# Linear attention beside an MLP: the kv blocks in 60-feature groups on half tiles, and the last rows of M copied by two DMA queues

## The chip, the cores and the metric

The kernel runs on one core of a Trainium2 chip. The metric is the device time of one execution in microseconds, from the start of the program to its end. The kernel before takes 263.5 us, the median of 3 runs that lie between 263.39 and 263.82 us.

The core has four engines that compute: TensorE (PE in the profile, its weight loads PEld), VectorE (DVE), ScalarE (ACT) and GpSimd (POOL). A fifth, SyncE (SP), only issues transfers. SP, ACT and POOL can each start DMA transfers from their own instruction stream, and each engine runs its own stream in order. Semaphores are the only tie between the engines.

## The reference: what is computed

There is one input x of 2048 tokens by 640 features in bfloat16. Two branches use it, and a gate per token mixes them.

```python
def _A_ref(x, wqkv, wo):                       # H = 32 heads of Dh = 20 features
    qkv = ((x @ wqkv).reshape(B, S, 3, H, Dh)).transpose(2, 0, 3, 1, 4)
    q, k, v = qkv[0], qkv[1], qkv[2]
    phi = lambda t: jnp.where(t > 0, t + 1, jnp.exp(t)) + 1e-6
    pq, pk = phi(q), phi(k)
    kv = jnp.einsum("bhsd,bhse->bhde", pk, v)  # one 20 x 20 block per head
    z = jnp.einsum("bhsd->bhd", pk)
    num = jnp.einsum("bhqd,bhde->bhqe", pq, kv)
    den = jnp.einsum("bhqd,bhd->bhq", pq, z)[..., None] + 1e-6
    return (num / den).transpose(0, 2, 1, 3).reshape(B, S, D) @ wo

def _B_ref(x, w1, w2, w3, w4):                 # F = 1728
    h = _gelu(_layernorm(x) @ w1)
    # four quarters of h are shifted by 1, -1, 2, -2 tokens
    x1 = x + shifted(h) @ w2
    return x1 + _gelu(_layernorm(x1) @ w3) @ w4

g = _sigmoid((x * gate_w).sum(-1, keepdims=True))
return g * a + (1 - g) * b
```

## The kernel before, in words

**Branch A without a pass over the values.** The kernel never forms v. Since kv = pk^T (x wv), it first builds GT, the 640 x 640 product of x and pk over the tokens (`gt_step`, L795), and then multiplies it with wv. Only the 20 x 20 blocks on the diagonal of that product are wanted, one per head. Then the blocks of kv are folded into the output projection: M is the block-diagonal kv times wo, 640 x 640, so that the attention output of a token tile is one matrix product of the normalised pq with M (`a_tile`).

**The kv stage.** `kvt_group` (L950) makes the diagonal of the product in groups of R6 = 120 features, that is six heads: five groups of 120 and one of 40. Each group is 5 matmuls over the contraction, 30 in all, in two work items ("kvt", 0) and ("kvt", 1) of 20 and 10. A matmul loads 128 columns of wv as its weights and moves 120 columns of GT. `lt_evac` multiplies each group in PSUM with a mask of 20 x 20 blocks on VectorE and writes it to Lt. For each of the six groups `m_group` (in order 5, 0, 1, 2, 3, 4) then makes 120 rows of M with two matmuls, of 512 and 128 columns (L613 with Lt and wo_aug as operands), and ScalarE copies them out of PSUM (L669).

**Where the last 40 rows of M go.** The five 120-row groups fill partitions 0 to 119 of the five blocks of `M_sb`. The 40 rows of group 5 go to partitions 120 to 127 of the blocks, eight to each. An engine cannot move rows across partitions, so ScalarE copies group 5 to `Mt`, and `m_tail` (item ("mt",)) copies it from there by 5 DMAs of 8 rows each on SP's queue (L286). `a_tile` for token tile 0 waits for all of them. `qn_scale` writes the normalised pq in the same order of features (L1063), and `qt_tile` turns it to features by tokens with a DMA transpose on SP (L282).

**What sets the order.** Every operation is recorded by a small scheduler. The work is cut into items with costs, streams and dependencies; a planner (`_Items.run`) picks the next item by the earliest time that its model gives, and so writes out a fixed order for every engine before the program runs. Waits between engines follow from the memory that operations read and write. PSUM has eight banks, and `bank` and `pair` hand out the ones that the model expects to be free first; `bank_hold` keeps banks from being handed out. SP's stream is one queue in that order: the DMA transposes of the normalised tokens ("t1", u) and ("t2", u), those of pq ("qt", t), the five copies of ("mt",), the weight loads and the stores. ("t2", u) waits for GpSimd's normalisation of tile u (L635), and that waits for a slot of the three-deep buffer xn, so for the transpose three tiles earlier.

**The stretch around the change.** After GT, PE does the first MLP of branch B (w1 with xnT, w2 with hsT) and then the second (w3 with xnT into h2T, w4). The kv matmuls stand among the w1 groups, the M matmuls among the w2 and w3 groups. A w3 group is 5 matmuls of 512 columns (`w3_group`) that ScalarE empties with a gelu. Twenty w3 groups stand before the first `a_tile`; after it `a_tile` 1 to 3 alternate with further w3 groups.

**Half tiles elsewhere in the kernel.** `w3_half` (L1036) already runs two matmuls side by side, each on 64 of the 128 columns of the array, and `w4_half` (L1104, L1101) two matmuls on 64 of the 128 rows each.

Of the kernel before, what the change touches and what calls it, by code (L numbers as in the profile page):

```python
# [21 lines left out]
NK = D + 4  # L22
R6 = 120

# [405 lines left out]
def _build(nc, A_x, A_wqkv, A_wo, B_w1, B_w2, B_w3, B_w4, gate_w, out, dbg=None, stop=None):  # L430
# [49 lines left out]
    ident = pa.alloc("ident", [128, 128], BF16)  # L480
    mask = pa.alloc("mask120", [128, 6, 20], BF16)
    mask_t = pa.alloc("mask_t", [128, 6, 20], BF16)
    negh = pa.alloc("negh", [128, 4], F32)
# [86 lines left out]
    def nfree(ap):  # L570
        n = 1
        for d_ in ap.shape[1:]:
            n *= d_
        return n
# [96 lines left out]
    def memset(engf, ap, val):  # L671
        return engf(lambda e: e.memset(ap, val), [], [ap])
# [63 lines left out]
    memset(pool, negh[:], -0.5)  # L736
    aselect(mask_t[0:120], ones_c[0:120, 0:120].rearrange("p (b d) -> p b d", b=6), [[-20, 6], [0, 20]], ALU.is_ge, 0, 1)
    aselect(mask[0:120], mask_t[0:120], [[20, 6], [0, 20]], ALU.is_ge, 19, -1)
# [194 lines left out]

    kv_bank = {}

    def kvt_group(h):
        b = pair()
        kv_bank[h] = b
        bank_hold.update((b, b + 1))
# [12 lines left out]
        pe(fn, [wvf[:, :], GT[:, :, :]], [ps[:, b, 0:480], ps[:, b + 1, 0:1]], cost=len(mms) * 60.0)  # L952

    def lt_evac(h):
        b = kv_bank[h]
        for q_, r in enumerate(range(4) if h == 0 else range(4, 6)):
            n = min(R6, D - R6 * r)
            src = ps[0:n, b, R6 * q_:R6 * q_ + n].rearrange("p (h m i) -> p h m i", m=5, i=4)
            msk = mask[0:n, 0:n // DH, :].rearrange("p h (m i) -> p h m i", i=4)
            if r < 5:  # L960
                dst = Lt[0:n, r, 0:n].rearrange("p (h m i) -> p h m i", m=5, i=4)
            else:
                dst = Lt[0:n, r, 0:n].rearrange("p (m h i) -> p h m i", m=5, i=4)
            tt(dve, dst, src, msk, ALU.mult)
        bank_hold.difference_update((b, b + 1))

    def m_group(r):
        n = min(R6, D - R6 * r)
        kr = R6 if r < 5 else 128
        b = pair()  # L970
        mm_group(ps[:, b, 0:512], [(Lt[0:kr, r, :], wo_aug[0:kr, r, 0:512])])
        mm_group(ps[:, b + 1, 0:128], [(Lt[0:kr, r, :], wo_aug[0:kr, r, 512:D])])
        src = psf[0:n, 512 * b:512 * b + D]
        dst = M_sb[0:n, r, :] if r < 5 else Mt[0:n, :]
        activation(dst, src, ACTF.Copy)

    def m_tail():
# [73 lines left out]
    def qn_scale(t):  # L1051
        sd = qn_slot[t]
        ts(dve, dnr[:, 0, sd, :], dnr[:, 0, sd, :], EPS_PHI, None, ALU.add, ALU.bypass)
        dve(lambda e: e.reciprocal(dnr[:, 1, sd, :], dnr[:, 0, sd, :]), [dnr[:, 0, sd, :]], [dnr[:, 1, sd, :]], cost=350.0)
        blk = pq_tok[:, t, :].rearrange("p (j c) -> p j c", c=128)
        main = (blk[:, :, 0:R6].rearrange("p j (a d) -> p j a d", d=DH),
                pq_tok[:, t + 1, 0:5 * R6].rearrange("p (j a d) -> p j a d", a=6, d=DH),
                dnr[:, 1, sd, 0:30].rearrange("p (j a) -> p j a", a=6).unsqueeze(3).to_broadcast([128, 5, 6, DH]), 850.0)
        tail = (blk[:, :, R6:128].rearrange("p m (h i) -> p h m i", i=4),
                pq_tok[:, t + 1, 5 * R6:D].rearrange("p (h m i) -> p h m i", h=2, i=4),  # L1060
                dnr[:, 1, sd, 30:32].unsqueeze(2).unsqueeze(3).to_broadcast([128, 2, 5, 4]), 150.0)
# [114 lines left out]
    IT.add("MISC", ("w3load",), 0.0, w3_load, deps=[(("k", NT - 1), 0.0), (("t1", NT - 1), 0.0)])  # L1176
    IT.add("MISC", ("w4load",), 0.0, w4_load, deps=[(("kvt", 1), 0.0), (("t1", NT - 1), 0.0), (("z", NT - 1), 1.5)])
    for c in range(NCH):
        for j in range(KFF):
            deps = []  # L1180
            if c == 0 and j == 0:
                deps0 = [(("kvt", 1), 0.0), (("z", NT - 1), 1.5)]
            else:
                deps0 = []
# [95 lines left out]
```

## Time and profile before

| what | value |
|---|---|
| median of 3 runs | 263.5 us |
| the profiled execution, its own time | 263.69 us |
| its span from the first to the last instruction | 261.6 us |
| DVE busy | 149.0 us, 57% of the span |
| ACT busy | 106.8 us, 41% |
| POOL busy | 95.3 us, 36% |
| DMA, mean | 95 GB/s |
| granted TensorE clock | 1.000 |

A row of the timeline gives start, duration, engine, line, operation and tiles, then how many instructions were merged; in brackets stands the idle time before it and what ended it. A row of SPq or ACTq is the issue of a transfer, and its duration is the time that the issuing queue was occupied, not the time until the data landed. The chain of waits is the list of pieces that led to the last instruction, in order of time. L613, L643, L669 and L286 are lines of helpers that record matmul groups, VectorE tensor operations, ScalarE activations and transfers, so a row of theirs is told apart by its tiles. A matmul's duration in a row includes the way through the array; the pace is read from the starts.

### The profile page before, as it was taken

To read this page: it belongs to the slowest core of one execution; us is meant where nothing else is said; L and a number is where in the kernel's file an instruction comes from. 1 tells how busy PE (TensorE), PEld (TensorE's weight loads), DVE (VectorE), ACT (ScalarE), POOL (GpSimd) and SP (SyncE) were. 2 spreads that over 40 slices of the span, in tenths; PEclk is the share of its full clock that TensorE was granted. 3 is DMA by queue.
4 is the path that set the end of the run, shared out by engine and by line. 5 is a ranking of instruction groups with operands and counts; after the bars stand their busy time and mean duration, and the time that the engine had idled before them with its cause. 6 is when DMAs were issued, how large, how long until landed. Compare 5 with 4: busy or idle time off the path is not lost.

```text
span 261.6 us, 4268 instructions
## 1 busy us (share of the span) xinstructions
PE 256.0 (98%) x1668; PEld 135.7 (52%) x1699; DVE 149.0 (57%) x267; ACT 106.8 (41%) x215; POOL 95.3 (36%) x150
## 2 busy tenths in 40 slices
PE   8999999999999999999999999999999999999996
PEld 4555555555555555554444545554455544455553
DVE  2497787899903699979995407992023410143332
ACT  1386767752355756684875140005500045100000
POOL 5003996849774018687753201230011100011000
PEclk9999999999999999999999999999999999999999
DMA  6885979660566895544766600232000020000211
GB/s 198 253 91 137 165 172 172 179 122 16 87 125 103 224 387 155 76 81 74 111 124 125 103 0 0 41 84 77 0 3 0 3 100 0 3 0 0 103 50 50
DMA packets 50612, 24.82 MB, mean 95 GB/s; under 512 B 41973, under 2 KB 49182, under 8 KB 50593
## 3 DMA queue, kind: packets, MB, share of 16 engines
q1 hardware_dynamic: 49152, 20.98, 36.6%
q0 software_dynamic: 1152, 3.28, 5.7%
q8 instruction: 13, 0.21, 0.3%
q10 hardware_dynamic: 288, 0.30, 0.3%
q14 instruction: 7, 0.05, 0.1%
HBM read 12.04 MB, written 2.62 MB: 56 GB/s over the span
## 4 chain that ended last, share of the span: by engine, by line
PE 95%; DVE 1%; DMA 1%; issue 1%; ACT 0%
PE ps L613 60%; PE ps L1122 21%; PE ps L795 8%; PE ps L874 2%; DMA x_tok<-in_A_x_dram 1%; PE ps L1036 1%; PE ps L1104 1%; DVE x_tok L652 1%; PE ps L875 1%; PE ps L624 1%; PE ps L950 1%; DVE abx L652 0%; ACT junk L668 0%; DVE xT L678 0%; PE ps L1101 0%
## 5 line engine op out<-in xcount | busy, mean ns | idle before, releaser
L613 PE MATMUL ps<-xnT,w 128*128 128x512 bf16 x348 | 80.7, 379 | 0.7 <-issue 0.2
L1122 PE MATMUL ps<-w,h2T 128*128 128x512 bf16 (+1 forms) x411 | 58.1, 298 | 0.3
L669 ACT ACTIVATE h2T<-ps 128x512 bf16<-128x512 f32 x52 | 30.4, 600 | 65.7 <-PE ps L613 65.7
L613 PEld LDWEIGHTS ps<-xnT,w 128*128 128x128 bf16 x360 | 34.0, 98 | 36.9 <-issue 0.4
L652 DVE SCALAR_TENSOR_TENSOR x_tok<-ps,stg,abx 128x512 bf16<-128x512 f32 (+1 forms) x32 | 17.2, 550 | 61.6 <-PE ps L1122 61.6
L635 POOL TENSOR_SCALAR abx<-x_tok,stg 128x640 f32<-128x640 bf16 x16 | 14.8, 927 | 101.9 <-DVE x_tok L652 95.1
L1122 PEld LDWEIGHTS ps<-w,h2T 128*128 128x128 bf16 x416 | 32.4, 98 | 25.6 <-issue 1.1
L635 POOL TENSOR_SCALAR xn<-x_tok,st 128x640 bf16<-128x640 bf16 x32 | 33.8, 1062 | 15.3 <-DMA xnT<-xn 14.8
L669 ACT ACTIVATE Er<-ps 128x640 bf16<-128x640 f32 x32 | 22.3, 705 | 18.7 <-PE ps L875 8.6
L668 ACT ACTIVATE junk<-x_tok 128x640 bf16<-128x640 bf16 x32 | 23.6, 737 | 4.8 <-DVE x_tok L650 4.3
L669 ACT ACTIVATE hsT<-ps 128x512 bf16<-128x512 f32 (+1 forms) x32 | 18.9, 594 | 15.1 <-PE ps L613 14.8
L613 PE MATMUL ps<-M_sb,pqnT 128*128 128x512 bf16 (+1 forms) x157 | 23.7, 297 | 0.2
L613 PE MATMUL ps<-w,hsT 128*128 128x128 bf16 (+1 forms) x158 | 23.7, 298 | 0.1
L795 PE MATMUL ps<-pk_tok,x_tok 128*128 128x128 bf16 (+1 forms) x156 | 23.3, 297 | 0.2
L652 DVE SCALAR_TENSOR_TENSOR abx<-ps,stg,abx 128x640 f32<-128x640 f32 x16 | 14.1, 884 | 14.6 <-PE ps L613 14.6
L613 PE MATMUL ps<-wkg,xT 128*128 128x131 bf16 (+1 forms) x148 | 22.4, 298 | 0.1
L613 PEld LDWEIGHTS ps<-w,hsT 128*128 128x128 bf16 x160 | 13.3, 98 | 12.3
L613 PEld LDWEIGHTS ps<-M_sb,pqnT 128*128 128x128 bf16 x160 | 13.1, 98 | 10.4
L613 PE MATMUL ps<-wq,xT 128*128 128x128 bf16 (+1 forms) x118 | 18.1, 298 | 0.1
L650 DVE SCALAR_TENSOR_TENSOR x_tok<-ps,x_tok 128x640 bf16<-128x640 f32 x16 | 13.1, 821 | 6.9 <-PE ps L613 6.0
L613 PEld LDWEIGHTS ps<-wkg,xT 128*128 128x128 bf16 x150 | 12.2, 98 | 9.0
L795 PEld LDWEIGHTS ps<-pk_tok,x_tok 128*128 128x128 bf16 x160 | 12.4, 98 | 8.4
(70 smaller groups left out, 231.8 us busy)
## 6 DMA issues: line engine op xcount, KB each, us to landing
w<-in_B_w_dram SPq DMA_DIRECT2D x1, 2160.0 KB, 8.5
w<-in_B_w_dram SPq DMA_DIRECT2D x1, 2080.0 KB, 14.1
x_tok<-in_A_x_dram SPq DMA_DIRECT2D x3, 640.0 KB, 5.8
out_dram<-x_tok SPq DMA_DIRECT2D x3, 640.0 KB, 3.5
w<-in_B_w_dram POOLq DMA_DIRECT2D x8, 160.0 KB, 5.1
wkg<-in_A_wqkv_dram SPq DMA_DIRECT2D x5, 160.0 KB, 4.1
wv<-in_A_wqkv_dram POOLq DMA_DIRECT2D x1, 800.0 KB, 6.2
wo_aug<-in_A_wo_dram POOLq DMA_DIRECT2D x5, 150.0 KB, 5.2
```

What stands on the lines that cost most here:

```text
L613: ins = e.matmul(out_ap, l, r, start=(i == 0), stop=(i == n - 1))
L624: ins = e.transpose(o, s_, ident[:])
L635: return engf(lambda e: e.tensor_scalar(out_ap, in_ap, s1, s2, op0, op1), rd, [out_ap], cost=cost)
L650: return dve(lambda e: e.scalar_tensor_tensor(out_ap, in0, scalar, in1, op0, op1, accum_out=accum), rd, [out_ap, accum], cost=cost + 70.0)
L652: return dve(lambda e: e.scalar_tensor_tensor(out_ap, in0, scalar, in1, op0, op1), rd, [out_ap], cost=cost)
L668: return act(lambda e: e.activation(out_ap, in_ap, func, bias=bias, scale=scale, accum_out=accum), rd, wr, cost=cost)
L669: return act(lambda e: e.activation(out_ap, in_ap, func, bias=bias, scale=scale), rd, wr, cost=cost)
L795: ins = e.matmul(o, l, r, start=(t0 + q_ == 0), stop=(t0 + q_ == NT - 1))
L874: e.matmul(ps[:, b, 0:512], l, w[:, k, 0:512], start=(k == 0), stop=(k == KD - 1))
L875: return e.matmul(ps[:, b + 1, 0:n2], l, w[:, k, 512:512 + n2], start=(k == 0), stop=(k == KD - 1))
L950: ins = e.matmul(o, l, r_, start=st_, stop=sp_, skip_group_check=True)
L1122: ins = e.matmul(o, l, r, start=False, stop=(i == KFF - 1), skip_group_check=(n0 > 0))
```

## The change

The features are taken in groups of R3 = 60 (three heads) instead of 120: ten groups of 60 and one of 40. Two groups stand side by side, one on partitions 0 to 59 and one on 64 to 123; `PAIRS` names them.

- `kvt_group` becomes one item of 55 matmuls, of 64 columns of weights each: 50 that move 60 columns and 5 that move 40. The two groups of a pair write the two halves of the same PSUM bank, and all six pairs share one bank.
- `lt_evac` becomes four VectorE multiplications in place of six.
- Lt holds four slots of 60 columns and one full slot; `m_group` is used for group 5 and for slot 4 (all 128 rows). The other eight groups are done by the new `m_quads`: 16 matmuls on tiles of 64 x 64, eight of 512 columns and eight of 128. They take six single PSUM banks, held together, and ScalarE empties them with four copies of 512 columns and two of 256.
- M has groups of 60 rows and then 4 rows from group 5 in each half of a block. `m_tail` so becomes ten DMAs of 4 rows, five on SP's queue and five on ACT's, alternating, and depends on ("mq",) instead of on ("m", 5), since the copies out of PSUM now write all 128 partitions of M_sb.
- `load_wvo` loads wo by seven DMAs on GpSimd's queue in place of six, and the whole of wo_aug is set to zero at the start (3840 columns in place of 640). The mask is made by four selects and one addition in place of two selects.
- `qn_scale` writes 10 x 60 and 10 x 4 features in place of 5 x 120 and 5 x 8.

The core of the diff:

```diff
-R6 = 120
+R3 = 60
+PAIRS = ((0, 2), (1, 3), (4, 6), (5, 7), (8, 9), (10,))
...
     def load_wvo():
...
-        for r in range(6):
-            n = min(R6, D - R6 * r)
-            sch.dma("pool", wo_aug[0:n, r, :], A_wo[R6 * r:R6 * r + n, :], "wo", group_total=6, deps=dp)
+        for c, r, g, m in ((0, 0, 0, 2), (1, 0, 2, 2), (0, 2, 4, 2), (1, 2, 6, 2), (0, 4, 8, 1), (1, 4, 9, 1)):
+            sch.dma("pool", wo_aug[64 * c:64 * c + R3, r:r + m, :],
+                    A_wo[R3 * g:R3 * (g + m), :].rearrange("(g p) d -> p g d", p=R3), "wo", group_total=7, deps=dp)
+        sch.dma("pool", wo_aug[0:D - 10 * R3, 5, :], A_wo[10 * R3:D, :], "wo", group_total=7, deps=dp)
...
-    memset(pool, wo_aug[:, 5, :], 0.0)
     memset(pool, hsT[:, :, 0:4], 0.0)
     memset(pool, hsT[:, :, S:S + 4], 0.0)
+    memset(pool, wo_aug[:], 0.0)
...
-    def kvt_group(h):
-        b = pair()
...
+    def kvt_group():
+        b = bank()
+        kv_bank.append(b)
+        bank_hold.add(b)
         mms = []
-        for q_, r in enumerate(range(4) if h == 0 else range(4, 6)):
-            n = min(R6, D - R6 * r)
+        for r, gs in enumerate(PAIRS):
             for k in range(KD):
-                mms.append((ps[:, b, R6 * q_:R6 * q_ + n], wvf[:, D * k + R6 * r:D * k + R6 * r + 128], GT[:, k, R6 * r:R6 * r + n],
-                            q_ == 0 and k == 0, k == KD - 1))
+                for c, g in enumerate(gs):
+                    n = min(R3, D - R3 * g)
+                    mms.append((ps[64 * c:64 * c + 64, b, R3 * r:R3 * r + n], wvf[:, D * k + R3 * g:D * k + R3 * g + 64],
+                                GT[:, k, R3 * g:R3 * g + n], r == 0 and k == 0, k == KD - 1))
...
+    def m_quads():
+        held = [bank() for _ in range(6)]
+        bs, bt = held[:4], held[4:]
+        bank_hold.update(held)
...
+        for i in range(2):
+            jobs = []
+            for h in range(2):
+                rows = slice(64 * h, 64 * h + 64)
+                for c in range(2):
+                    jobs.append((ps[64 * c:64 * c + 64, bs[2 * i + h], :], Lt[rows, 2 * i + c, 0:64],
+                                 wo_aug[rows, 2 * i + c, 0:512], True))
+            quad(jobs, [ps[:, bs[2 * i + h], :] for h in range(2)])
...
+        for j in range(4):
+            activation(M_sb[:, j, 0:512], ps[:, bs[j], :], ACTF.Copy)
+        for h in range(2):
+            activation(M_sb[:, h:4:2, 512:D], ps[:, bt[h], 0:256].rearrange("p (i n) -> p i n", n=128), ACTF.Copy)
+        bank_hold.difference_update(held)
+
     def m_tail():
-        for j in range(KD):
-            sch.dma("sp", M_sb[R6:128, j, :], Mt[8 * j:8 * j + 8, :], "mt", group_total=KD)
+        for s_ in range(2 * KD):
+            p0 = 64 * (s_ % 2) + R3
+            sch.dma(("sp", "act")[s_ % 2], M_sb[p0:p0 + 4, s_ // 2, :], Mt[4 * s_:4 * s_ + 4, :], "mt", group_total=2 * KD)
...
-    for h in range(2):
-        IT.add("KVF", ("kvt", h), 0.0, lambda h=h: kvt_group(h), deps=[(("g", KD - 1), 1.0)])
-        IT.add("KVF", ("lt", h), 0.0, lambda h=h: lt_evac(h), deps=[(("kvt", h), 0.0)])
-    for n, r in enumerate((5, 0, 1, 2, 3, 4)):
-        IT.add("KVF", ("m", r), 0.0, lambda r=r: m_group(r), deps=[(("lt", 1), 1.0), (("w3", (1 + 3 * n) // KFF, (1 + 3 * n) % KFF), 0.0)])
-    IT.add("MT", ("mt",), 0.0, m_tail, deps=[(("m", 5), 1.5), (("t1", NT - 1), 0.0)])
+    IT.add("KVF", ("kvt",), 0.0, kvt_group, deps=[(("g", KD - 1), 1.0)])
+    IT.add("KVF", ("lt",), 0.0, lt_evac, deps=[(("kvt",), 0.0)])
+    IT.add("KVF", ("m", 5), 0.0, lambda: m_group(5), deps=[(("lt",), 1.0), (("w3", 0, 1), 0.0)])
+    IT.add("KVF", ("m", 4), 0.0, lambda: m_group(4), deps=[(("w3", 0, 3), 0.0)])
+    IT.add("KVF", ("mq",), 0.0, m_quads, deps=[(("w3", 0, 6), 0.0)])
+    IT.add("MT", ("mt",), 0.0, m_tail, deps=[(("mq",), 1.5), (("t1", NT - 1), 0.0)])
...
-        deps = [(("qt", t), 3.0), (("w4load",), 0.0), (("m", KD - 1), 1.0), (("mt",), 2.5)]
+        deps = [(("qt", t), 3.0), (("w4load",), 0.0), (("mq",), 1.0), (("mt",), 2.5)]
```

Where the planner puts the pieces, as the built programs have them:

| engine | before | after |
|---|---|---|
| PE, kv | 20 kv matmuls, one w1 group, 10 kv matmuls | 55 kv matmuls in one piece |
| PE, M | group 5 among the w2 tiles; then 7 w3 groups, m0, 1 group, m1, 3 groups, m2, 2 groups, m3, 3 groups, m4, 2 groups, `a_tile` 0 | group 5 at the same place; then 6 w3 groups, slot 4, 2 groups, the 16 quad matmuls, 10 groups, `a_tile` 0 |
| SP | transposes t2 0 to 7, the five copies of mt, t2 8 to 11, qt 0 to 5, t2 12 to 15, qt 6 and on | t2 0 to 11, qt 0 to 5, t2 12 to 14, five copies of mt, t2 15, qt 6 and on |
| ACT | no transfer in this stretch | the other five copies of mt, four w3 groups' gelus behind the copies of the quads |

More of the change, by code (lines that the diff above doesn't have):

```diff
@@ L951, in fn @@
             return ins
[L952 to L965, printed above, removed]
+        pe(fn, [wvf[:, :], GT[:, :, :]], [ps[:, b, 0:6 * R3]], cost=1100.0)
@@ new lines, in lt_evac @@
+    def lt_evac():
+        b = kv_bank[0]
+        n = D - 10 * R3
+        tt(dve, Lt[0:n, 5, 0:n], ps[0:n, b, 5 * R3:5 * R3 + n], mask[0:n, 0:n], ALU.mult)
+        tt(dve, Lt[:, 0:4, 0:R3], ps[:, b, 0:4 * R3].rearrange("p (r d) -> p r d", d=R3),
+           mask[:, :].unsqueeze(1).to_broadcast([128, 4, R3]), ALU.mult)
+        for c in range(2):
+            rows = slice(64 * c, 64 * c + 64)
+            tt(dve, Lt[rows, 4, 64 * c:64 * c + R3], ps[rows, b, 4 * R3:5 * R3], mask[rows, :], ALU.mult)
+        bank_hold.discard(b)
@@ L967, in m_group @@
     def m_group(r):
-        n = min(R6, D - R6 * r)
-        kr = R6 if r < 5 else 128
         b = pair()
-        mm_group(ps[:, b, 0:512], [(Lt[0:kr, r, :], wo_aug[0:kr, r, 0:512])])
-        mm_group(ps[:, b + 1, 0:128], [(Lt[0:kr, r, :], wo_aug[0:kr, r, 512:D])])
+        mm_group(ps[:, b, 0:512], [(Lt[:, r, :], wo_aug[:, r, 0:512])])
+        mm_group(ps[:, b + 1, 0:128], [(Lt[:, r, :], wo_aug[:, r, 512:D])])
+        n = 128 if r < 5 else D - 10 * R3
         src = psf[0:n, 512 * b:512 * b + D]
-        dst = M_sb[0:n, r, :] if r < 5 else Mt[0:n, :]
+        dst = M_sb[:, 4, :] if r < 5 else Mt[0:n, :]
@@ L1054, in qn_scale @@
         dve(lambda e: e.reciprocal(dnr[:, 1, sd, :], dnr[:, 0, sd, :]), [dnr[:, 0, sd, :]], [dnr[:, 1, sd, :]], cost=350.0)
[L1055 to L1060, printed above, removed]
+        blk = pq_tok[:, t, :].rearrange("p (s c) -> p s c", c=64)
+        main = (blk[:, :, 0:R3].rearrange("p s (a d) -> p s a d", d=DH),
+                pq_tok[:, t + 1, 0:10 * R3].rearrange("p (s a d) -> p s a d", a=3, d=DH),
+                dnr[:, 1, sd, 0:30].rearrange("p (s a) -> p s a", a=3).unsqueeze(3).to_broadcast([128, 10, 3, DH]), 850.0)
+        tail = (blk[:, :, R3:64].rearrange("p (h m) i -> p h m i", m=5),
+                pq_tok[:, t + 1, 10 * R3:D].rearrange("p (h m i) -> p h m i", h=2, i=4),
                 dnr[:, 1, sd, 30:32].unsqueeze(2).unsqueeze(3).to_broadcast([128, 2, 5, 4]), 150.0)
```

36 lines of the change are left out of this document (27 added, 9 removed).

## The prediction

> **What bounds the kernel now.** I read the page first, then the chain of waits around the change, then SP's queue.
>
> ```profile
> PE 256.0 (98%) x1668; PEld 135.7 (52%) x1699; DVE 149.0 (57%) x267; ACT 106.8 (41%) x215; POOL 95.3 (36%) x150
> PE 95%; DVE 1%; DMA 1%; issue 1%; ACT 0%
> ```
>
> PE is busy for 98% of the span and is 95% of the chain. The chain where the M work stands shows the same in detail:
>
> ```profile
> 132.16 9.90 PE ps L613 x51
> ...
> 142.12 8.34 PE ps L613 x49
> ```
>
> PE runs on without waiting for anyone. So PE time saved comes off the span one for one, and so does any new wait of PE come on top. The question is what PE saves, and whether it must now wait. SP's queue from 117 us on decides the second half:
>
> ```profile
> 117.55 3.49 SPq L286 DMA_DIRECT2D M_sb<-Mt  x5
> 121.08 5.63 SPq L282 DMA_TRANSPOSE xnT<-xn  x4
> 126.75 7.89 SPq L282 DMA_TRANSPOSE pqnT<-pq_tok  x6
> 135.17 5.17 SPq L282 DMA_TRANSPOSE xnT<-xn  x4
> 140.40 7.88 SPq L282 DMA_TRANSPOSE pqnT<-pq_tok  x6
> ```
>
> SP is occupied from 117.55 to 148 us almost without a gap: a transpose holds it for 1.29 to 1.41 us (5.17 / 4, 5.63 / 4; 7.89 / 6 = 1.32), and the five copies of M's last rows for 3.49 us, early, in a lull. Here is when PE needs those rows:
>
> ```profile
> 140.55 1.52 PE L613 MATMUL ps<-M_sb,pqnT 128*128 128x512 bf16 x10
> ```
>
> The first `a_tile` starts at 140.55, 19.5 us after the last copy was issued. The change spends this reserve: the copies move behind 4 + 6 + 3 transposes.
>
> **The PE work that changes.**
>
> ```profile
> 77.85:78.90 1.05, 1.05 (x20) 0.88 (x17) 1.00 0.54 102
> 79.97:80.40 0.43, 0.39 (x10) 0.28 (x7) 1.00 0.54 102
> 127.30 0.44 PE L613 MATMUL ps<-wo_aug,Lt 120*128 120x512 bf16 x2
> 127.57 1.24 PE L613 MATMUL ps<-xnT,w 128*128 128x512 bf16 x5
> 149.22 1.24 PE L613 MATMUL ps<-xnT,w 128*128 128x512 bf16 x5
> 150.39 2.35 PE L1036 MATMUL ps<-xnT,w 128*64 128x512 bf16 x20
> 154.94 0.39 PE L1104 MATMUL ps<-w,h2h 64*128 64x512 bf16 x2
> 155.16 0.22 PE L1101 MATMUL ps<-w,h2h 64*128 64x128 bf16 x2
> 155.44 0.22 PE L1101 MATMUL ps<-w,h2h 64*128 64x128 bf16 x2
> 155.59 0.61 PE L1122 MATMUL ps<-w,h2T 128*128 128x512 bf16 x2
> ```
>
> kv before: 1.05 + 0.39 = 1.44 us; 20 matmuls of 120 columns take 0.0525 each, so of the second piece's 0.39 five take 0.26 and the five of 40 columns 0.026 each. Half-array matmuls in this kernel do run side by side: 20 of 512 columns (L1036) take 2.35, of which 0.38 is the last one's own way through the array, so (2.35 - 0.38) / 9 = 0.22 a pair, while a single one of 512 columns takes 0.216 ((1.24 - 0.38) / 4). If a pair of 60 columns takes the 0.026 of the short ones, kv after is 30 x 0.026 = 0.79; if nothing overlaps it is 55 x 0.026 = 1.43. A change of array shape costs something: 149.22 + 5 x 0.216 = 150.30, and L1036 starts at 150.39, so 0.09; from 155.44 to 155.59 it is 0.15 where 0.055 would do, so 0.1 again. Two changes make 0.2. kv thus gains 0.45 or loses 0.19; I take a gain of 0.4, since both half-shape rows show overlap.
>
> The Trainium skill speaks against this gain. TensorEngine Tiling (Array Packing), section Instruction Overhead, gives each matmul an overhead of some 60 cycles, so that one of 1 column is as long as one of 60, and warns not to tile a dimension that is already small. By it kv would come to 55 x 0.025 + 0.2 = 1.58 and lose 0.14 (an estimate); whether the overheads of two tiles overlap no row here shows.
>
> M before: 127.57 - 127.30 = 0.27 a group, six make 1.63. After: two full groups 0.54, then quads. If four tiles run together, 2 x 0.216 + 2 x 0.055 = 0.54 and two shape changes 0.2: a gain of 0.35. If only two run together, 1.08 + 0.2: a loss of 0.19. L1036 shows pairs by columns and L1104 with L1101 pairs by rows; both at once is not shown, but nothing in either is shared. The quads need six banks at once, and in this stretch ScalarE is behind (below), so the last pair, which reuses slot 4's banks, may wait some 0.3 for its copy. I take a gain of 0.3 in all, bounds +0.35 and -0.5. Sum: PE reaches `a_tile` 0 some 0.7 us sooner, at 139.85.
>
> **When the copies land.** GpSimd sets when SP may start on t2 8.
>
> ```profile
> 119.77 2.61 POOL L635 TENSOR_SCALAR xn<-x_tok,st 128x640 bf16<-128x640 bf16 x3
> 130.87 3.81 POOL L635 TENSOR_SCALAR xn<-x_tok,st 128x640 bf16<-128x640 bf16 x3
> xnT<-xn SPq DMA_TRANSPOSE x32, 2.7
> out_dram<-x_tok SPq DMA_DIRECT2D x1, 32.0 KB, 1.6
> 4.55 2.33 SPq L286 DMA_DIRECT2D wkg<-in_A_wqkv_dram  x5
> ```
>
> Normalised tile 8 is ready at 119.77 + 0.88 = 120.65 (or up to 0.4 sooner, by kv's gain), so with the copies gone from in front t2 8 can start only 0.4 to 0.8 sooner than its 121.08. From there 13 transposes follow: at 1.32 they take 17.1 us; before, the same 13 took from 121.08 to 135.17 + 3 x 1.32 = 139.12, so 18.0. None waits for data: tile 11 needs t2 8 landed, about 120.5 + 2.7 + 0.88 = 124.1, and its turn is at 124.4; tiles 12 to 14 are ready from 131.75 to 134.68, and their turns come from 133.7 on. So SP comes to its first copy between 120.25 + 17.1 = 137.4 and 120.65 + 18.0 = 138.7; I take 137.9. Five copies held SP for 3.49 before, 0.62 to 0.78 each; plain loads take 0.43 (2.33 for five), so 2.25 at least, if four rows rather than eight make it quick. I keep 3.49, the row of the same copy. The last is issued at 137.9 + 2.87 = 140.8. No row shows its landing; a small store takes 1.6, a transpose 2.7. I take 1.9, nearer to the plain copy. So M is whole at 142.7, against 140.55 when `a_tile` 0 started before: **+2.1 us**. PE waits 2.8 us and its own gain is lost in that wait. The bounds: 137.4 + 4 x 0.45 + 1.6 = 140.8 (+0.2), and 138.7 + 2.87 + 2.7 = 144.3 (+3.7).
>
> ACT's five copies don't come last:
>
> ```profile
> 259.18 0.35 ACTq L286 DMA_DIRECT2D out_dram<-x_tok  x1
> 126.21 3.02 ACT L669 ACTIVATE h2T<-ps 128x512 bf16<-128x512 f32 x6
> 132.86 0.70 ACT L669 ACTIVATE M_sb<-ps 120x640 bf16<-120x640 f32 x1
> 127.30:140.60 13.30, 13.25 (x66) 6.18 (x66) 12.38 (x24) 10.55 (x19) 8.60 (x10) 1.00 0.62 119
> ```
>
> ACT starts its backlog at 126.21 with 0.5 per gelu: seven of them, slot 4 (0.7), the quads' six copies (some 3, by 0.70 for 640 columns) and four gelus more bring it to about 135.4; then five issues, of 0.35 as ACT's other one to 0.78 as SP's slowest copy, so the last lies between 137.2 and 139.3 at its end and has landed by 139.1 to 142.0. ACT is busy 10.55 of 13.3 us there; five issues add 1.8 to 3.9 and delay gelus by as much. PE has eight banks and the delayed gelus are used later, and they catch up while PE waits: nothing on the path; 0.6 for a late gelu if banks ran out.
>
> **The rest, hidden.** VectorE does four mask products for six, and `qn_scale` moves the same 600 and 40 elements; DVE is not on the chain here. t2 15 and qt 6 onward leave SP some 2 us later; the next users are L1036 at 150.39, and `a_tile` 4 after that; both are later too. GpSimd has one more wo load and a longer memset at the start:
>
> ```profile
> 48.18 3.32 POOL L286 DMA_DIRECT2D wo_aug<-in_A_wo_dram  x6
> 55.14 0.27 POOL L635 TENSOR_SCALAR st<-lr 128x4 f32<-128x4 f32 x1 [2.71 <-ACT lr L669]
> 2.59 0.74 POOL L672 MEMSET Lt<- 128x768 bf16 x1
> 3.38 0.63 POOL L672 MEMSET wo_aug<- 128x640 bf16 x1
> 18.93 0.26 POOL L635 TENSOR_SCALAR st<-lr 128x4 f32<-128x4 f32 x1 [14.81 <-ACT lr L669]
> 5.81 1.02 DVE L678 COPY xT<-ps 128x640 bf16<-128x640 bf16 x2 [0.78 <-PE ps L624]
> 120.78 0.78 DVE L635 TENSOR_SCALAR dnr<-dnr 128x32 f32<-128x32 f32 x1
> 125.36 0.17 DVE L635 TENSOR_SCALAR dnr<-dnr 128x32 f32<-128x32 f32 x1
> ```
>
> The load costs 3.32 / 6 = 0.55 and falls into the 2.71 that GpSimd waits next. By the two memsets (0.11 for 128 columns) 3840 columns take 3.3 us, to about 7.4, beside VectorE's copies at 5.81 that PE awaits. GpSimd's next work is at 18.9, so itself it costs nothing. But VectorE can be held by GpSimd: the small operation at 120.78 took 0.78, the same one at 125.36 only 0.17. Held likewise, the copies would come up to 1.6 late. Against it: these copies read PSUM and the stretched operation does not; of reads from PSUM I found none stretched. I take 0, and keep the 1.6 as a rival.
>
> **The rivals.**
> 1. *The copies land in time* (faster). Then PE's 0.7 stays: 262.8. It decides at a landing before 139.9, so SP's first copy by 135.1 even with my figures, or 137.1 with the shortest issue and landing. The 13 transposes would need some 1.1 us each instead of 1.32, and no group of rows has less than 1.29. 7 in 100. Landing at 140.8 to 141.0, about as before, 6 in 100: 263.5.
> 2. *The wait is longer.* ACT's issues at about the same time as SP's could slow both queues, which no row shows, and the hiccups of 0.9 in the 13 transposes repeat: 144.3, so 267.2. If PE stands for long the clock may also fall; PE started the program slowly, and it stood 3.2 us at the end:
>
> ```profile
> 0.83 2.72 PE L847 MATMUL ps<-const-bfloat16-1.0 128*128 128x512 bf16 x6 [0.83 <-PEq L1265]
> 258.40:261.60 3.20, 0.68 (x13) 1.00 0.17 51
> ```
>
>    Six matmuls of 512 columns took 2.72 there, twice the later pace, and the clock stayed 1.00 through 3.2 idle us. A fall would cost about as much as that start, 2.72 - 6 x 0.216 = 1.4 on top: 268.6. 12 in 100 together. The Trainium skill, TensorE: Matmul & The Clock Gate, section Part 1: The HAM clock gate, puts the fall after one idle window of about 3.4 us; the end of this trace agrees as far as it goes, and by that rule a wait of 2.8 us is safe and one of 4.4 us is not.
> 3. *The memset holds VectorE* at the start: everything 1.6 later on top, 267.2. 5 in 100.
>
> **How the numbers follow.** The profiled execution is 263.69 us, 2.1 outside its span of 261.6, and 0.19 over the median 263.5. With +2.1 it is 265.8, and 265.6 against the median. This case has 70 in 100, with 264.6 to 266.6 as its own range (copy issues from 0.45 to 0.78, SP at 137.4 to 138.7). A measurement of this kernel tells about 0.2%, 0.53 us, from no change. Faster 0.07, same 0.06, slower 0.87 (70 + 12 + 5). The range leaves out rival 1 and the worst of rival 2: 264.1 to 267.5.
>
> **What would show it.** PE should stand for 2 to 3.5 us just before its first matmul with M_sb and pqnT, with M_sb<-Mt as the releaser; SP's copies should start at about 138 behind three xnT transposes. kv should take about 1.0 with its shape changes, the quads about 0.75. I am wrong if that first matmul starts before 140.5, if kv or the quads take as long as before, or if PE is already late at 10 us.

## The result, and the profile after

The changed kernel takes 265.28 us, the median of 7 runs (265.01 to 267.5), against 263.53 for the kernel before, measured beside it. The ratio is 1.009, with a 95% interval from 1.0068 to 1.0113: slower, by 1.75 us in the medians (three longer executions lift the ratio above the 1.0066 of the medians). The profiled execution took 265.10 us, 0.18 under the median, with a span of 263.1.

PE in the timeline of the changed kernel, around the M work (the columns are start, duration, engine, line, operation and tiles, count, and in brackets the idle time before it with what ended it):

```profile
125.72 2.32 PE L614 MATMUL ps<-xnT,w 128*128 128x512 bf16 x10
127.97 0.80 PE L991 MATMUL ps<-wo_aug,Lt 64*64 64x512 bf16 x16
128.96 10.97 PE L614 MATMUL ps<-xnT,w 128*128 128x512 bf16 x50 [0.18 <-ACT h2T L670]
142.08 1.53 PE L614 MATMUL ps<-M_sb,pqnT 128*128 128x512 bf16 x10 [2.16 <-DMA M_sb<-Mt]
```

The last row answers to the row 140.55 of before: `a_tile` 0 now starts with an idle PE in front of it, and the copies of M's last rows end it. By the starts, the last w3 matmul began at 139.54 and needs 0.22, so PE was ready at 139.76 and stood 2.32 us. SP's queue and ScalarE's say why:

```profile
114.99 10.20 SPq L283 DMA_TRANSPOSE xnT<-xn  x5
125.24 7.89 SPq L283 DMA_TRANSPOSE pqnT<-pq_tok  x6
133.22 3.90 SPq L283 DMA_TRANSPOSE xnT<-xn  x3
137.57 3.30 SPq L287 DMA_DIRECT2D M_sb<-Mt  x5
140.98 1.24 SPq L283 DMA_TRANSPOSE xnT<-xn  x1
```

```profile
129.22 2.68 ACT L670 ACTIVATE M_sb<-ps 128x512 bf16<-128x512 f32 x6
133.49 3.76 ACTq L287 DMA_DIRECT2D M_sb<-Mt  x5
```

What the copies wait for, the quads' output, left ScalarE by 132; SP comes to them at 137.57, behind the three xnT transposes, over five us later, and ScalarE's five had been issued by 137.25. The chain of waits goes through SP's last issue to the landing, and from there along PE:

```profile
140.30 1.74 DMA M_sb<-Mt
142.03 0.05 issue
142.08 9.92 PE ps L614 x60
```

The kv matmuls, and the start:

```profile
76.11 1.24 PE L614 MATMUL ps<-xnT,w 128*128 128x512 bf16 x5
77.28 1.13 PE L958 MATMUL ps<-GT,wv 128*64 128x60 bf16 x55
78.34 1.90 PE L614 MATMUL ps<-xnT,w 128*128 128x512 bf16 x8
```

```profile
4.97 0.72 PE L625 MATMUL ps<-ident,x_tok 128*128 128x128 bf16 x10
6.00 0.39 PE L881 MATMUL ps<-wq,xT 128*128 128x512 bf16 x1 [0.31 <-DVE xT L679]
...
11.89 0.38 PE L881 MATMUL ps<-wkg,xT 128*128 128x512 bf16 x1
```

The start in the kernel before:

```profile
5.03 1.27 PE L624 MATMUL ps<-ident,x_tok 128*128 128x128 bf16 x10
6.36 0.48 PE L874 MATMUL ps<-wq,xT 128*128 128x512 bf16 x1
...
12.38 0.38 PE L874 MATMUL ps<-wkg,xT 128*128 128x512 bf16 x1
```

This is where the time went, from the starts on PE in the two profiled executions: wkg starts at 11.89 against 12.38 (-0.49, at the start, ahead of all that was edited in PE's order); kv and its two changes of shape take 1.15 against 1.44 (-0.29); the M work takes 1.62 against 1.63; the wait adds 2.32; from `a_tile` 0 to the end it is 121.06 against 121.05. The sum is +1.54, and the spans differ by 1.5. The first term goes with the granted clock: the trace's clock record has full speed from 4.89 us on here and from 6.58 us on before, and the ten transposes of x that lie between take 0.72 and 1.27 us.

In three of the seven runs the record shows a mean granted clock of 0.994 and 267.2 to 267.5 us, in the other four 1.00 and 265.0 to 265.3. The seven of the kernel before lie between 263.39 and 263.84. What that is comes with the experiments on the clock.

### The profile page after: what moved, and what is told of

The parts are those of the page before. It is cut to its first block, busy times and chain, and to the rows that moved or that the text cites. A ratio compares the mean times of both kernels' runs of the same rounds, so it can differ in the third digit from the quotient of the medians.

```text
span 263.1 us, 4373 instructions
## 1 busy us (share of the span) xinstructions
PE 256.7 (98%) x1732; PEld 134.2 (51%) x1732; DVE 147.6 (56%) x265; ACT 106.3 (40%) x217; POOL 100.1 (38%) x154
## 4 chain that ended last, share of the span: by engine, by line
PE 88%; DVE 5%; ACT 2%; DMA 2%; ACTq 1%; SPq 0%; issue 0%; DVEq 0%
PE ps L614 53%; PE ps L1163 21%; PE ps L802 8%; PE ps L881 2%; ACT h2T L670 2%; DVE x_tok L651 2%; ACTq L287 1%; DMA x_tok<-in_A_x_dram 1%; PE ps L1077 1%; PE ps L1145 1%; DVE pq_tok L1104 1%; DVE x_tok L653 1%; DMA M_sb<-Mt 1%; DVE dnr L1087 1%; DVE qprod L644 1%; PE ps L882 1%
## 5 line engine op out<-in xcount | busy, mean ns | idle before, releaser
L614 PE MATMUL ps<-xnT,w 128*128 128x512 bf16 x360 | 81.6, 379 | 0.2 <-ACT h2T L670 0.2
L1163 PE MATMUL ps<-w,h2T 128*128 128x512 bf16 (+1 forms) x416 | 58.8, 299 | 0.0
L636 POOL TENSOR_SCALAR xn<-x_tok,st 128x640 bf16<-128x640 bf16 x32 | 35.8, 1126 | 13.1 <-DMA xnT<-xn 12.7
L614 PE MATMUL ps<-M_sb,pqnT 128*128 128x512 bf16 (+1 forms) x160 | 24.4, 299 | 2.2 <-DMA M_sb<-Mt 2.2
L802 PE MATMUL ps<-pk_tok,x_tok 128*128 128x512 bf16 (+1 forms) x160 | 23.9, 299 | 0.0
L614 PE MATMUL ps<-w,hsT 128*128 128x512 bf16 (+1 forms) x160 | 23.9, 299 | 0.0
L614 PE MATMUL ps<-wkg,xT 128*128 128x512 bf16 (+1 forms) x150 | 22.6, 299 | 0.0
L614 PE MATMUL ps<-wq,xT 128*128 128x512 bf16 (+1 forms) x120 | 18.3, 299 | 0.0
```

The lines of the kernel that those rows point to most:

```text
L614: ins = e.matmul(out_ap, l, r, start=(i == 0), stop=(i == n - 1))
L636: return engf(lambda e: e.tensor_scalar(out_ap, in_ap, s1, s2, op0, op1), rd, [out_ap], cost=cost)
L802: ins = e.matmul(o, l, r, start=(t0 + q_ == 0), stop=(t0 + q_ == NT - 1))
L1163: ins = e.matmul(o, l, r, start=False, stop=(i == KFF - 1), skip_group_check=(n0 > 0))
```

## The experiments

The theory: PE stands because SP issues its five copies some five us later than their data allow, and nothing else in the change costs time. The rivals: the loss is in the edits themselves (quads, ScalarE's issues and the gelus behind them); and a clock that falls in the wait. Each kernel was timed beside the kernel before (263.6 to 263.7 in all three sessions).

### SP's copies ahead of t2 12

```diff
-        IT.add("T2", ("t2", u), ..., deps=[(("n2", u), 1.1)])
+        IT.add("T2", ("t2", u), ..., deps=[(("n2", u), 1.1)] + ([(("mt",), 0.0)] if u == 12 else []))
```

> The changed kernel, with transpose t2 12 made to wait in SP's order for the ten copies of M's last rows, so that SP's five copies stand ahead of t2 12 to 14 in place of behind them; nothing else moves. Theory (PE waits for rows that SP issues too late): SP's first copy starts where t2 12 did, at about 133.2 us, the last is issued at 136.6, landed at 138.4, before PE comes to the first matmul with M_sb at 139.8. The 2.3 us wait is gone, the median is 265.28 - 2.3 = 263.0 (262.7 to 263.4). t2 12 to 15 leave SP some 3.4 us later and nobody waits for them. Rival (the time is lost in the edits themselves: in the quads, in ScalarE's five issues and the gelus behind them): 264.7 or more, with the gap in PE still there. Rival (the clock): if the runs of 267.2 us of the changed kernel come from the wait, no run here shows a granted clock under 1.00.

Measured: 263.81 us, ratio 1.000 (0.9979 to 1.0021), 12 runs, no clock under 0.999. Moving three transposes gives back nearly all of the loss, but 0.8 more stays than expected. PE, SP and ScalarE in its timeline:

```profile
129.85 10.74 PE L614 MATMUL ps<-xnT,w 128*128 128x512 bf16 x49 [0.41 <-ACT h2T L670]
141.21 1.03 PE L614 MATMUL ps<-M_sb,pqnT 128*128 128x512 bf16 x4 [0.62 <-DMA M_sb<-Mt]
```

```profile
134.01 3.30 SPq L287 DMA_DIRECT2D M_sb<-Mt  x5
137.84 5.55 SPq L283 DMA_TRANSPOSE xnT<-xn  x4
```

```profile
134.16 4.29 ACTq L287 DMA_DIRECT2D M_sb<-Mt  x5
```

```profile
137.71 3.22 DMA M_sb<-Mt
```

(The record of the first matmul with M_sb is missing. Its weights were loaded at 140.98, and by the starts PE was ready at 140.43, so it stood about 0.6.) SP is through at 137.3 as planned, but ScalarE's five issues, now at the same time as SP's, take 4.29 instead of 3.76, the last begins at 137.71, and by the chain (last row) its data are there at 140.93: 3.2 us for one copy, with SP's transposes behind it from 137.84. So the second queue, harmless in the changed kernel, is the last one here.

### The kernel before with its copies late

```diff
-    IT.add("MT", ("mt",), 0.0, m_tail, deps=[(("m", 5), 1.5), (("t1", NT - 1), 0.0)])
+    IT.add("MT", ("mt",), 0.0, m_tail, deps=[(("m", 5), 1.5), (("t2", 14), 0.0)])
```

and t2 15 waits for ("mt",).

> The kernel before, with only its five copies of M's last rows moved on SP's queue, from ahead of t2 8 to behind t2 14. Theory: SP's first copy starts at 137 to 138, five take 3.3 to 3.5, the last lands some 1.7 after its issue, so at about 142.4; PE comes to its first matmul with M_sb at 140.55 as before and waits 1.9: 265.4 (264.8 to 266.0). This is the wait alone, without new kv, quads or ScalarE copies. Rival (a late row is hidden, the loss is in the new matmuls or copies): 263.5.

Measured: 266.68, 268.04, 270.56 and 272.01 us, ratio 1.0167 (1.0107 to 1.0227). The order on SP alone, with the old kv and M, is enough for the loss. Its size was missed: the fastest run, at clock 1.00, is 3.1 over the kernel before and not 1.9, and no trace of that run was taken. The profiled one is the slowest:

```profile
115.98 13.16 SPq L282 DMA_TRANSPOSE xnT<-xn  x5
...
141.48 3.52 SPq L286 DMA_DIRECT2D M_sb<-Mt  x5
```

```profile
146.25 2.31 PE L613 MATMUL ps<-M_sb,pqnT 128*128 128x512 bf16 x5 [5.80 <-DMA M_sb<-Mt]
```

Five transposes take 13.16 us here against 10.20 above: one of them held SP for 2.95. PE stands 6.0 us, and the five matmuls behind that take 2.31 us, half speed. Once a queue of transposes is on the path, such a hold-up goes into the time.

### All ten copies behind t2 15

```diff
-    IT.add("MT", ("mt",), 0.0, m_tail, deps=[(("mq",), 1.5), (("t1", NT - 1), 0.0)])
+    IT.add("MT", ("mt",), 0.0, m_tail, deps=[(("mq",), 1.5), (("t2", NT - 1), 0.0)])
```

> The changed kernel with the ten copies behind t2 15 too, one transpose (1.24 us) later on SP. Theory of the wait: PE stands 2.3 + 1.24 = 3.5 us; 266.5 where the granted clock stays at 1.00. Theory of the clock (three of seven runs of the changed kernel show 0.994 and 267.2 to 267.5 because the idle stretch makes the clock fall): with a longer stretch nearly every run falls, at 268.6 with a clock of about 0.99, and the page shows PE at half speed just behind the wait. If those runs have nothing to do with the wait, most runs lie at 266.5 and no more fall than before. If late rows aren't the cause at all: 265.3.

Measured: 272.16 us (272.01 to 272.29), ratio 1.0308 (1.0275 to 1.0342); clock 0.987 in all four runs. The edit did more than was meant: with the item later in the planner's order, ScalarE's five copies came later too, from 140.56, so PE waits for these:

```profile
146.58 0.13 PEld L614 LDWEIGHTS ps<-M_sb,pqnT 128*128 128x128 bf16 x2 [6.56 <-DMA M_sb<-Mt]
```

```profile
146.98 1.49 PE L614 MATMUL ps<-M_sb,pqnT 128*128 128x512 bf16 x3 [6.47 <-DMA M_sb<-Mt]
```

The first matmul with M_sb has no record; it began when its weights were loaded, at 146.58. PE was ready at 140.35, so the wait is 6.2 us and not 3.5, and the next three matmuls of 512 columns have taken 1.49 with their way through the array: half speed. As a test of 3.5 us the run failed; as a long wait it is used below.

### Two w3 groups more ahead of `a_tile` 0

```diff
-            deps.append((("w3", 1, t + 6), 0.0))
+            deps.append((("w3", 1, t + 8), 0.0))
...
-            if c == 1 and 7 <= j <= 10:
-                deps.append((("a", j - 7), 0.0))
+            if c == 1 and 9 <= j <= 12:
+                deps.append((("a", j - 9), 0.0))
```

> The changed kernel with a_tile 0 to 3 two w3 groups later in PE's order (22 groups ahead of a_tile 0 in place of 20); SP's queue as in the changed kernel. Theory: the two groups (10 matmuls, 2.16 us) fill the wait; PE comes to the first matmul with M_sb at 139.76 + 2.16 = 141.9, against rows landed at 142.0: 265.28 - 2.2 = 263.1 (262.8 to 263.5), with the copies exactly as late as in the changed kernel. Rival (the lateness costs elsewhere too, in w3 groups or in w4 behind a_tile 3, or the loss is in the edits themselves): 264.5 to 265.3.

Measured: 263.50 us, ratio 0.9991 (0.9964 to 1.0018), 10 runs, no clock under 0.999. SP's copies are as late as in the changed kernel, from 137.83:

```profile
129.40 12.90 PE L614 MATMUL ps<-xnT,w 128*128 128x512 bf16 x58 [0.41 <-ACT h2T L670]
142.33 1.53 PE L614 MATMUL ps<-M_sb,pqnT 128*128 128x512 bf16 x10
```

`a_tile` 0 starts as late as before, 142.33, but PE has done two groups more by then and stands only 0.2 us. Late rows cost only what PE has no other work for. The 0.4 that are missing against the expectation are that 0.2 and probably two changes of shape more (0.09 each), since `w3_half` 0 and 2 now stand apart with an `a_tile` between them.

### The changed kernel again, and SP's share one transpose later

```diff
-    IT.add("MT", ("mt",), 0.0, m_tail, deps=[(("mq",), 1.5), (("t1", NT - 1), 0.0)])
+    IT.add("MT", ("mta",), 0.0, lambda: m_tail(1), deps=[(("mq",), 1.5), (("t1", NT - 1), 0.0)])
+    IT.add("MTS", ("mt",), 0.0, lambda: m_tail(0), deps=[(("mta",), 0.0), (("t2", NT - 1), 0.0)])
```

with m_tail(h) doing every second copy; the first of the two runs has no edit.

> The changed kernel once more, beside the three below. Theory of the wait: 265.0 to 265.5 where the granted clock stays at 1.00. Theory of the clock: where a run shows 0.994, it is 1.7 to 2.2 longer, and if the profiled execution is one of these, PE stands longer than the 2.3 us seen so far (a transpose on SP was held up) and goes at half speed for a while behind the wait. If PE stands 2.3 us there too and the clock falls all the same, the fall doesn't hang on the length of the wait; if the half-speed stretch lies elsewhere, the wait isn't its cause.

> The changed kernel with SP's five copies one transpose later, behind t2 15, and ScalarE's five where they are. Theory of the wait: SP's first copy at 138.9 in place of 137.6, the last landed at 143.3, PE stands 3.6 us: 266.5 (266.2 to 267.0) where the clock stays. Theory of the clock: at 3.6 us some or most runs fall to 0.994 or below and are about 2 us longer, 268 to 269. If ScalarE's copies or the quads were the cause: 265.3, as the changed kernel.

Measured: the changed kernel 266.11 us (265.14 to 267.44), ratio 1.0079 (1.0052 to 1.0107), one of seven runs at 0.994. Its profiled execution, 266.38, has the same wait of 2.32 us; the rest is a stall of about 1 us at 43 us, for a transpose of x, far ahead of the kv and M work:

```profile
143.39 1.53 PE L614 MATMUL ps<-M_sb,pqnT 128*128 128x512 bf16 x10 [2.15 <-DMA M_sb<-Mt]
```

SP's share one transpose later: 266.78, 269.69, 269.7 and 270.5, ratio 1.0184 (1.0126 to 1.0242), three of four runs at 0.994 or below. In the profiled one PE was ready at 140.15 and stood until 143.97, so 3.82 against 3.6 expected. The rows of PE by stretches of 3.41 us (busy time and count, granted clock, DMA share, GB/s):

```profile
139.34:142.75 3.41, 0.97 (x5) 1.00 0.29 53
142.75:146.16 3.41, 2.19 (x6) 0.50 0.51 99
146.16:149.58 3.42, 3.42 (x14) 0.50 0.60 117
149.58:153.00 3.42, 3.42 (x25) 1.00 0.68 80
```

PE goes at half speed for two such stretches, 1.2 us of which it stands. That costs (149.58 - 143.97) / 2 = 2.8 us beyond the wait: 263.2 without a wait (the kernels with the rows right behind the quads, below) + 3.8 + 2.8 = 269.8, and the run took 269.7. The longer wait above closes the same way: clock at half to 152.07, so (152.07 - 146.58) / 2 = 2.7, and 263.2 + 6.2 + 2.7 = 272.1 against 272.16.

### The clock once more

> The changed kernel once more, for the granted clock against the length of the wait: with 2.3 us 4 of 14 executions showed 0.994, with 3.8 us 3 of 4 were at 0.994 or below, with 6.6 us 4 of 4. Theory of the clock (the fall depends on how much of one fixed stretch of 3.4 us PE stands idle, and the stretch begins at another point in each execution): again some 2 to 4 of 10 show 0.994, and these are 1.7 to 2.2 us longer than the rest, which lie at 265.0 to 266. If the fall came from other things than this wait, the kernels without it show it as often.

Measured: 266.59 us (264.86 to 267.77), ratio 1.0101 (1.0065 to 1.0137); three of six runs at 0.994, at 267.2 to 267.8. The profiled execution, 267.77, is one of them. The landing of the last copy, the load of the weights, and PE by stretches:

```profile
141.40 1.74 DMA M_sb<-Mt
```

```profile
143.18 0.13 PEld L614 LDWEIGHTS ps<-M_sb,pqnT 128*128 128x128 bf16 x2 [2.66 <-DMA M_sb<-Mt]
```

```profile
139.64:143.05 3.41, 1.38 (x7) 1.00 0.03 10
143.05:146.46 3.41, 2.87 (x11) 0.50 0.66 126
146.46:149.87 3.41, 3.41 (x20) 1.00 0.91 119
```

Here too the record of the first matmul with M_sb is missing; the last row landed at 143.14, and the weights were loaded at 143.18. The last w3 matmul began at 140.64, so PE was ready at 140.85 and stood 2.33 us, as long as in the two other traces of this kernel. The half-speed stretch is one of 3.41 us and begins just ahead of the end of the wait. It costs (146.46 - 143.18) / 2 = 1.6 us, and PE had come to the wait 1.1 us later than in the first profile: 265.1 + 1.1 + 1.6 = 267.8.

In all four traces with a fall the half speed begins inside the wait, and falls are more frequent with the longer waits. Over all runs of the experiments the clock was at 0.994 or below

- in none of 66 runs of the kernel before;
- in 1 of 58 runs of the kernels with the rows early or `a_tile` two groups later, whose traces show waits of 0 to 0.6 us; that one run, 267.75 us, has no trace;
- in 7 of 20 runs of the changed kernel, with 2.32 or 2.33 us in its three traces;
- in 3 of 4 at 3.8 us, 3 of 4 of the kernel before with its copies late (6.0 us in its trace), and 4 of 4 at 6.2 us.

In each record the edges of full and half speed lie on a grid of 3.41 us, at another place in each execution. What tells the executions with equal waits apart is where the wait lies on it. The clock held where PE stood 1.7 us within one stretch of the grid (the first profile, 139.76 to 141.42) and 1.8 us (the second, 141.55 to 143.39). It fell where PE stood 2.2 us within one stretch (the profile above, 140.85 to 143.05), 2.6 us (140.15 to 142.72, SP's share later), and a whole stretch (the two longest waits). A limit between 1.8 and 2.2 us in one stretch would fit all six traces. That is read off after the fact and not tested, so the exact rule stays open. So does part of the excess in runs without a trace: in the first session the three at 0.994 are 1.9 to 2.5 us longer than the other four, more than the 1.7 that one stretch at half speed can cost.

### The rows right behind the quads

```diff
-    IT.add("MT", ("mt",), 0.0, m_tail, deps=[(("mq",), 1.5), (("t1", NT - 1), 0.0)])
+    IT.add("MT", ("mt",), 0.0, m_tail, deps=[(("mq",), None), (("t1", NT - 1), 0.0)])
...
-        IT.add("QT", ("qt", t), ..., (("t2", 11 if t < 6 else NT - 1), 0.0)])
+        IT.add("QT", ("qt", t), ..., (("t2", 11 if t < 6 else NT - 1), 0.0)] + ([(("mt",), 0.0)] if t == 5 else []))
```

> The changed kernel with all ten copies right behind the quads' copies: on ScalarE ahead of the gelus of w3 (0,10) to (1,0) in place of behind them, on SP between qt 4 and t2 12 (qt 5 goes behind t2 14). Theory: both queues start at 132.4 and are through at about 136; no transpose is issued before the last copy has landed, so it lands 1.7 us after its issue (ScalarE's last one in the run with the rows ahead of t2 12 took 3.1, with a transpose issued in between), at 137.5, two us ahead of PE. The wait is gone: 0.30 under the kernel before, that is 263.2 to 263.4 against 263.6. Rival: the five issues (3.5 us) now delay four gelus that PE's banks need, and PE stands 0.5 to 1 us among the w3 groups: 263.8 to 264.3. Rival: the 0.8 us left in that run wasn't from ScalarE's late last copy but stays: 263.8.

> The rows right behind the quads once more, beside the others: 263.1 (262.8 to 263.3), 0.3 to 0.6 under the kernel before, and PE's first matmul with M_sb follows the w3 group ahead of it without a gap.

Measured: 263.08 us (262.79 to 264.37, and one at 267.75), ratio 0.9967 (0.9947 to 0.9987); the second time 263.36 (262.58 to 264.72), ratio 0.999 (0.9974 to 1.0007). SP, and PE, in the first:

```profile
131.91 3.40 SPq L287 DMA_DIRECT2D M_sb<-Mt  x5
```

```profile
129.06 10.96 PE L614 MATMUL ps<-xnT,w 128*128 128x512 bf16 x50 [0.18 <-ACT h2T L670]
139.86 1.52 PE L614 MATMUL ps<-M_sb,pqnT 128*128 128x512 bf16 x10
```

No gap is left ahead of `a_tile` 0, and the gelus that ScalarE does 3.9 us later stop nobody. From wkg to `a_tile` 0 PE needs 127.87 us, just what the changed kernel needs to be ready for it, against 128.17 before. The change without its wait is thus worth 0.3 us; the two measurements are 0.58 and 0.29 under the kernel before, the second within what can be told from no change. The one run at 267.75 (clock 0.994) has no trace.

### The quads two groups later as well

```diff
-    IT.add("KVF", ("mq",), 0.0, m_quads, deps=[(("w3", 0, 6), 0.0)])
+    IT.add("KVF", ("mq",), 0.0, m_quads, deps=[(("w3", 0, 8), 0.0)])
```

on top of the kernel above; SP's copies come between t2 12 and t2 13.

> The rows right behind the quads, and the quads two w3 groups later, with SP's five copies between t2 12 and t2 13. PE waited 0.25 us behind the quads for a bank that a late gelu held; ScalarE works off its backlog in two groups more. Theory: PE saves these 0.25, the last row lands at about 138.7, ahead of PE at 139.6: 262.8 to 262.9, against 263.08 with the rows right behind the quads. Rival: ScalarE's issues now start at 134 and the last row lands behind 139.6, so PE stands 0.5 us or more there: 263.3 to 263.8.

Measured: 262.86 us (262.5 to 264.81), ratio 0.997 (0.9951 to 0.9989), 12 runs, none below 0.999.

```profile
131.03 0.74 PE L991 MATMUL ps<-wo_aug,Lt 64*64 64x512 bf16 x16
131.70 8.81 PE L614 MATMUL ps<-xnT,w 128*128 128x512 bf16 x39
140.34 1.52 PE L614 MATMUL ps<-M_sb,pqnT 128*128 128x512 bf16 x10
```

From the first quad to the next w3 group it is 0.67 where the changed kernel needs 0.99, and no wait for ScalarE stands in front of the second row: the 0.3 was a wait for a bank. This version is faster than the kernel before by its interval, by 0.79 us in the medians.

### The price of kv's matmuls

```diff
+        mms = [m for r in range(6) for c in range(2 if r < 5 else 1) for m in mms[10 * r:10 * r + 10 if r < 5 else 55][c::2 if r < 5 else 1]] + mms
```

> The rows of M ahead of t2 12, and the 55 kv matmuls issued twice in one item: first with each group's five matmuls in a row (no two neighbours on different halves of the array), then in the order of the change (the two groups of a pair alternating). This leaves the work of kv doubled, for the price of the order alone. Theory (two tiles of 64 columns run side by side when they alternate): the first 55 take 50 x 0.026 + 5 x 0.018 = 1.4 us or more, the second 55 take 0.97 as in the changed kernel's trace. If a matmul of 60 columns has the same price alone or paired, both passes take 0.97; if the price is an overhead per matmul, both are equal too, and the pairing of tiles has no part in kv's gain.

Its first 55 matmuls, then its second 55, by the stretches on that line:

```profile
77.90:78.82 0.92, 0.92 (x55) 0.92 (x57) 1.00 0.52 101
78.83:79.81 0.98, 0.98 (x66) 0.98 (x58) 1.00 0.58 109
```

Both passes take nearly the same (0.92 and 0.98), so of the answers named beforehand the first, that the order matters, failed. (Each of these two kernels ran once, in 264.62 and 264.70 us, with the kv work doubled.) Whether the halves overlap was still open, and one more run put all on one half:

```diff
+                    one.append((ps[0:64, b, R3 * r:R3 * r + n],) + mms[-1][1:])
+        mms = one + mms
```

> The rows right behind the quads, and kv issued twice in one item: first all 55 matmuls on columns 0 to 63 of the array (the right half of each pair goes to the same place as the left and is thrown away), then the 55 as in the change. The work of kv is doubled, for the price alone. The order of the matmuls made no difference (0.91 us apart, 0.96 alternating), so either a matmul of 60 columns on half the array costs 0.0165 us by itself, or two halves run side by side whatever the order within ten matmuls. By the first, the first 55 take 0.9 to 1.0 us here too. By the second they go one behind another: 50 x 0.026 + 5 x 0.018 = 1.4 us or more, and the second 55 take 0.95.

```profile
77.79:79.49 1.70, 1.70 (x55) 1.70 (x56) 1.00 0.76 144
79.51:80.48 0.97, 0.97 (x62) 0.97 (x58) 1.00 0.55 108
```

On one half the 55 take 1.70, on both 0.97. The halves do run side by side, and within ten matmuls the order doesn't matter. A matmul of 60 columns on one half takes 1.70 / 54 = 0.0315 us, and the five of 40 columns are at the same pace.

## Why the prediction was right

The forecast was 265.6 us, from +2.1 by the wait; measured are 265.28, with the likeliest case and its own range (264.6 to 266.6) holding it. Step by step:

- *PE bounds the kernel, and a wait comes on top one for one*: right where the clock holds; where it falls, the wait costs 1.6 us and more besides. Behind `a_tile` 0 both executions take 121.05 and 121.06 us.
- *SP comes to its first copy at 137.9*: it came at 137.57, in an execution that began 0.49 sooner, so 0.16 behind the forecast by that. The 13 transposes took from 119.77 to 137.12, 17.35 for 17.1 to 18.0. Not foreseen were 0.45 us between the last transpose and the first copy.
- *Five copies hold SP 3.49, the last lands 1.9 after its issue*: 3.30, and 1.74.
- *ScalarE's copies don't come last*: right in the changed kernel, last issue over at 137.25 where 137.2 to 139.3 was given. It is by a small margin: with SP's copies early they are the last.
- *kv takes 0.99 with its changes of shape*: it takes 1.15, so the gain is 0.29 and not 0.4. The term that was off is "a pair of 60 columns takes the 0.026 of the short ones": one costs 0.0315 alone, and a pair about the same. The two changes of shape were 0.09 each. The rule of the Trainium skill that spoke against the gain (TensorEngine Tiling (Array Packing), section Instruction Overhead) would have given 1.58, and the traces don't bear that out as a sum. Its direction does show: 60 and 40 columns cost the same on a half. What it left open, whether two tiles' overheads overlap, the last run answers: they do.
- *M gains 0.3*: it gains 0.01, so one of the signs of being wrong that the prediction names, quads that take as long as before, came true. The quads do run four together (0.65 for 16, 0.54 worked out), but the wait for a bank, "some 0.3", which the value taken left nearly out, was there: 0.25 behind them and some of it inside. The version with the quads later shows the 0.67 without it.
- *PE is ready at 139.85*: 139.76, but by luck. Kv and M gave 0.30 for 0.7; 0.49 came from the start, where PE's first wq matmul at full pace stands at 6.00 instead of 6.36 and every engine shifts with it. That went with the granted clock, which came to full speed earlier in this execution. The three traces of the changed kernel alone have wkg between 11.89 and 12.30, so it can't be counted as a gain of the change. With it, wait and gain both come out smaller: 2.32 for 2.8, and 0.30 for 0.7.
- *Rival 1, the copies land in time*: no. The kernels with the rows early show what it would have given, 263.1 to 263.4; the 262.8 named for it needed the quads later too.
- *Rival 2, the wait is longer and the clock falls*: not the median, but 7 of 20 runs. The price named, 1.4, is near what one stretch at half speed cost (1.6). The rule of the Trainium skill cited beside it (TensorE: Matmul & The Clock Gate, section Part 1: The HAM clock gate) made a wait of 2.8 us safe; here a wait of 2.33 wasn't, so the measurement decides against it. Its length of about 3.4 us is right for the stretches, which begin and end 3.41 us apart in each record, but PE needn't stand for a whole one: 2.2 us of one were enough.
- *Rival 3, the memset holds VectorE*: no. The memset of 3840 columns ran as worked out, and VectorE's two copies beside it took less than before:

```profile
4.32 3.30 POOL L673 MEMSET wo_aug<- 128x3840 bf16 x1
```

```profile
5.45 0.89 DVE L679 COPY xT<-ps 128x640 bf16<-128x640 bf16 x2 [0.42 <-PE ps L625]
```

What made it right was asking where each moved issue stands in its queue, and when that queue comes to it, rather than when its data are ready: the data were there over five us sooner. What was weak was the small change on PE, which was right in its sum only by chance.

## What to carry to other kernels

When a change makes a late, small transfer depend on something new, look at what the planner puts ahead of it in its queue, and set the time of the queue against the time of the consumer; two edges of the graph were worth 2.3 us here, more than all the saved matmuls. Give a transfer that PE waits for a place ahead of bulk transposes, or give PE other work until it lands: both mend it. And a short wait of the engine that bounds the kernel cost another 70% of its length by the clock in some executions (1.6 us on 2.33, 2.8 on 3.82), so a mean over runs tells more here than one profile.

## What the runs showed of the hardware that was not expected

- The granted clock fell to half for 3.41 us after PE stood 2.3 us (2.2 of them ahead of the fall), and for 6.83 us after 3.8 or more; waits of 2.33 and 3.82 us thus cost 1.6 and 2.8 us more. Two other waits of 2.32 us, placed otherwise on the grid of 3.41 us, cost nothing more.
- Matmuls on different column halves overlap even if five of one half are issued ahead of five of the other (0.92 us for 55, against 1.70 on one half).
- A copy of 4 rows on SP's queue landed 1.74 us after its issue, with a transpose issued 0.69 us behind it. On ScalarE's queue the last one needed 3.22 us with a transpose of SP issued 0.13 us behind it, and 2.83 with one 0.6 us behind it. Why was not tried.
- In the changed kernel 0.45 us lie between SP's last transpose and its first copy. It isn't a price of that order: the copies follow a transpose after 0.05 us in the kernel with the rows right behind the quads, and there a like gap of 0.5 stands between two transposes instead. What it is stays open.
